# Decay on TensorE for three batches, and GpSimd in place of the DMA queue for the other five

## The chip, the cores and the metric

The kernel runs on one core of a Trainium2 chip. The metric is device time in microseconds. A core has engines that run side by side, each through its own list of instructions in order: TensorE (matrix products; PE in the profile, PEld its weight loads), VectorE (DVE), ScalarE (ACT), GpSimd (POOL) and SyncE (SP). In this kernel SP's queue starts most DMAs, and 16 DMA engines move the data. SBUF is the working memory with 128 partitions, PSUM the memory into which TensorE writes.

## The reference

Attention with a decay, then a gated product of the tokens with weights:

```python
scores = (1 / sqrt(64)) * q @ k.T                  # 8 batches, 8 heads, 576 positions, 64 wide
cum = cumsum(log(clip(f, 1e-4, 1.0)), axis=-1)     # one row of 576 for each of 64 heads
scores = where(j > i, -1e9, scores + cum[i] - cum[j])
attn = softmax(scores)                              # over j
x = (attn @ v), the heads side by side              # 4608 tokens x 512
out = ((x @ w_a) * (x @ w_b)) @ w_out               # 512 -> 1536 -> 512
```

Because the softmax is taken over j, the term cum[i] falls out, and only -cum[j] has to be added to a score. For that, the vector cum of a head has to be there on all the partitions that hold that head's queries: it has to be spread.

## The kernel before, in words

A batch is worked in four **pairs** of heads; pair number t runs from 0 to 31, so batch b has t = 4b to 4b+3, and a **unit** u is two pairs. The queries of a head fall into blocks i = 0 to 3 of 128 and a last one, i = 4, of 64. A block i sees the keys of blocks 0 to i.

For each unit TensorE forms the scores in four groups (`qk_group`, L379): blocks 1 and 0, block 2, block 3, block 4. What follows depends on the batch.

- **Batches 0 and 1** (`DIRECT = 2`): the decay is added by TensorE too, as matmuls with a one-column selector (`pick`) against rows of cum in fp16 (`crow`), and the causal mask by matmuls of `low` with `neg`, into the same PSUM tile (L398 to L428). VectorE then takes the row maximum from PSUM (`do_max`, L484), and ScalarE the exponential from PSUM (L537, L543).
- **Batches 2 to 7**: a DMA on SP's queue reads two rows of cum from `cum_d` in HBM and writes them to all 128 partitions of a buffer `spread` (`load_spread`, L451). GpSimd makes masked copies of it with three affine selects (L458, L464, L469). VectorE adds scores and spread decay and takes the extremum in one instruction for each block and head (`do_decay`, L508) into an SBUF tile `S`, from which ScalarE takes the exponential.

In both cases ScalarE also sums the rows, VectorE takes reciprocals (L550, L552), and GpSimd multiplies each block by them in place (`do_norm`, L560: a `tensor_scalar` whose scalar is a column of `st`). The normalised blocks are turned by TensorE in batch 0 and by transposing DMAs on SP's queue (L576) from batch 1 on; TensorE multiplies them with v (L604, L606, L616, L629) into `xT`. GpSimd also converts k, q and v (L141, L139) to fp16.

The second product is made in tiles of 256, 256, 256, 384, six times 512, and 384 tokens: for each of 12 blocks of 128 columns two groups of matmuls (`psa`, `psb`, L877), a copy of the one (ScalarE or VectorE) and VectorE's product (L888), and then the matmuls `pso` (L897). A tile needs the attention of all heads of its tokens.

The order is written out by hand: every step is an `op` with a number, `ORDER` lists all numbers, and `CHOICE` gives the engine where more than one may do it. An engine's own list is `ORDER` cut down to that engine, and nothing overtakes within it. In it TensorE's matmuls of the second product for earlier tokens stand between the attention steps of later batches. The last products with v (t = 30, 31) stand behind all but the last two token tiles of TensorE's list.

The cum rows themselves come from a start section (L190 to L226): f is loaded twice by two DMAs, once as the first 16 heads four times over on partitions 0 to 63, once as all 64 heads on partitions 64 to 127; then clip, logarithm, scan, and two VectorE steps and a copy that make the fp16 rows `crow` of high and low parts.

Of the kernel before, what the change touches and what calls it, by code (L numbers as in the profile page):

```python
# [37 lines left out]
def kernel(  # L38
# [30 lines left out]
    DIRECT = 2  # L69
    EARLY = 2  # L70
    PSPREAD = range(DIRECT * NP, EARLY * NP)
# [13 lines left out]
    lsel = fixed("lsel", [128, 1], FP32)  # L85
# [5 lines left out]
    crow = spare[1][:, 1536:1536 + S]  # L91
# [4 lines left out]
    chigh = wout16.rearrange("p n k -> p (n k)")[:, 4608:4608 + S]  # L96
# [21 lines left out]
    osb_pool = pool("osb", RING["osb"])  # L118
    ps = pool("ps", 1, space=bass.MemoryType.PSUM)
# [37 lines left out]
    def picks(_):  # L157
        nc.vector.tensor_reduce(out=lsel, in_=ident.rearrange("p (a x r) -> p x a r", x=2, r=16)[:, 1],
                                axis=AXXY, op=ADD, negate=True)
# [25 lines left out]
    def f_tiles():  # L185
        x = [s_pool.tile([128, 1024], FP32, tag="S", name=n) for n in ("cum_f", "cum_l")]
        cw["f"], cw["l"] = x[0][:, 0:S], x[1][:, 0:S]
# [15 lines left out]
    def clip(lo, hi):  # L203
        x = cw["f"][:, lo:hi]
        nc.vector.tensor_scalar(out=x, in0=x, scalar1=1e-4, scalar2=1.0, op0=MAX, op1=MIN)
# [4 lines left out]
    def scan(lo, hi):  # L210
        x = cw["f"]
        nc.vector.tensor_tensor_scan(out=x[:, lo:hi], data0=cw["1"][:, lo:hi], data1=cw["l"][:, lo:hi],
                                     initial=x[:, lo - 1:lo] if lo else 0.0, op0=MUL, op1=SUB)

    def high_part(lo, hi):
        nc.vector.tensor_copy(out=chigh[HP[0], lo:hi], in_=cw["f"][HP[0], lo:hi])

    def rows_part(lo, hi):
        nc.vector.scalar_tensor_tensor(out=crow[HP[0], lo:hi], in0=chigh[HP[0], lo:hi], scalar=lsel[HP[0]],
                                       in1=cw["f"][HP[0], lo:hi], op0=MUL, op1=ADD)  # L220

    def rows_again(e, lo, hi):
        ENG[e].tensor_copy(out=crow[HP[1], lo:hi], in_=crow[HP[0], lo:hi])

    def cum_store(_):
        nc.sync.dma_start(out=cum_d, in_=cw["f"][HP[1]])  # L226

    f_tiles()
    o_f = [op("AS", "ldf", lambda e, m=m: f_load(e, m), size=m) for m in range(2)]
    s_users = [take(o_f[0], "S") for _ in range(2)]  # L230
    o_f[1].after.append(o_f[0])
    o0 = op("D", "ones", f_ones, [])
    o0.after.append(o_f[0])
    o_w = op("A", "table", warm_table(LN), [o0])
    crow_ops, lns, mine = [], [], [o_f[1], o0]
    for lo, hi in ((0, 256), (256, S)):
        a = (lo, hi)
        o1 = op("D", "fclip", lambda _, a=a: clip(*a), o_f, hi - lo)
# [3 lines left out]
        o4 = op("D", "fhi", lambda _, a=a: high_part(*a), [o3], hi - lo)  # L242
        o5 = op("D", "frow", lambda _, a=a: rows_part(*a), [o4, o_pick], hi - lo)
        crow_ops.append(op("DP", "frow2", lambda e, a=a: rows_again(e, *a), [o5], hi - lo))
# [27 lines left out]
    def load_qk(b, which, hh):  # L272
        if b == 0 and hh:
            c = wout16.rearrange("p n k -> p (n k)")[:, 2304 * (which == "q"):2304 * (which == "q") + 2304]
            x = c.bitcast(FP32)
# [21 lines left out]
    def batch_inputs(b):  # L297
# [4 lines left out]
        for which, part, gm in items:  # L302
            gate = qk_ops[(2 * (b - 1) + gm // 4, gm % 4)][-1:] if b else []
# [17 lines left out]
            ld = op("S", "ldqk", lambda _, which=which, hh=hh: load_qk(b, which, hh))  # L321
# [3 lines left out]
            for lo, hi in (((0, 5), (5, TW)) if b == 0 else ((0, TW),)):  # L325
# [5 lines left out]
                else:  # L331
                    ca.deps.append(cas[0])
                    nx.append(ca)
                cas.append(ca)
            tp = op("D", "tqk", lambda _, which=which, hh=hh: transpose_qk(b, which, hh), cas)
# [3 lines left out]
            else:  # L339
                tp.deps.append(T_ops[(which, b, 0)])  # L340
# [6 lines left out]
    def weights():  # L347
# [8 lines left out]
        for nm, js, src, dst, n in items:  # L356
            o = op("P", "ldw", lambda _, src=src, dst=dst: nc.gpsimd.dma_start(out=dst, in_=src), size=n)
            if nm == "o":
                o.deps.extend([*crow_ops, T_ops[("q", 0, 1)], T_ops[("k", 0, 1)]])
# [19 lines left out]
    def qk_group(u, g):  # L379
        b, hh = divmod(u, 2)  # L380
        qT, kT = T[("T", "q", b)], T[("T", "k", b)]
        if single(u, g):
# [3 lines left out]
        heads = [(c[w] if g == 3 else [c[w][0], c[w][1]] if single(u, g) else [c[w][:, 0, :], c[w][:, 1, :]],  # L386
                  h, RG[2 * w + h], 8 * b + 4 * hh + 2 * w + h) for w in range(2) for h in range(2)]
# [4 lines left out]
        if g == 3:  # L392
# [4 lines left out]
            for x, lo, hi in ((0, 0, SF), (1, SF, S)):  # L397
                if b < DIRECT or (b < EARLY and x):  # L398
                    for y, h, r, n in heads:
                        mm(y[HP[h], x, 0:hi - lo], pick[r, n:n + 1].to_broadcast([32, 64]), crow[r, lo:hi], stop=True)  # L400
            if b < EARLY:
# [8 lines left out]
        for i in groups[g]:  # L410
# [718 lines left out]
```

## Time and profile before

| | us |
|---|---|
| median of three runs | 405.43 (403.7 to 407.23) |
| the profiled execution | 402.69 |
| its span, first to last instruction | 400.9 |
| TensorE busy | 378.9 (95%) |
| VectorE busy | 315.5 (79%) |
| GpSimd busy | 262.8 (66%) |
| ScalarE busy | 250.6 (63%) |
| moved by DMA | 80.71 MB, of which 24 spread loads of 576 KB |

The span is about 2 us shorter than the execution's own time. Busy time leaves out instructions that an engine's sequencer does by itself. In a row of the profile, L560 is line 560 of the kernel, "PA<-PA,st" the written and the read tiles, "x60" a count, then come the busy time in us and the mean of one in ns, and behind the bar the idle time of that engine just before these instructions. A row of a table of stretches gives, for each engine, its busy time within the stretch and the number of its instructions, then the granted TensorE clock, the share of the 16 DMA engines (queued packets count, so it can pass 1) and GB/s.

### The profile page before, as it was taken

To read this page: it belongs to the slowest core of one execution; us is meant where nothing else is said; L and a number is where in the kernel's file an instruction comes from. 1 tells how busy PE (TensorE), PEld (TensorE's weight loads), DVE (VectorE), ACT (ScalarE), POOL (GpSimd) and SP (SyncE) were. 2 spreads that over 40 slices of the span, in tenths; PEclk is the share of its full clock that TensorE was granted. 3 is DMA by queue.
4 is the path that set the end of the run, shared out by engine and by line. 5 is a ranking of instruction groups with operands and counts; after the bars stand their busy time and mean duration, and the time that the engine had idled before them with its cause. 6 is when DMAs were issued, how large, how long until landed. Compare 5 with 4: busy or idle time off the path is not lost.

```text
span 400.9 us, 10798 instructions
## 1 busy us (share of the span) xinstructions
PE 378.9 (95%) x3856; PEld 209.3 (52%) x3856; DVE 315.5 (79%) x958; ACT 250.6 (63%) x756; POOL 262.8 (66%) x438
## 2 busy tenths in 40 slices
PE   5679799989999999999999999999999999999996
PEld 5557575765846544444545454544454444444553
DVE  5879997979998988989899789899959893373450
ACT  2678895768768777758785777675868673310111
POOL 4988899787967796979696948697858753000000
PEclk9869999999999999999999999999999999999999
DMA  7999999999999999999899998999997827101102
GB/s 245 261 217 224 253 284 224 233 209 225 208 281 224 267 199 305 202 310 191 270 217 286 238 301 168 242 242 243 255 199 192 151 68 177 54 0 53 55 2 78
DMA packets 149466, 80.71 MB, mean 201 GB/s; under 512 B 130660, under 2 KB 133476, under 8 KB 149412
## 3 DMA queue, kind: packets, MB, share of 16 engines
q1 hardware_dynamic: 145492, 75.02, 79.1%
q0 software_dynamic: 3696, 4.72, 7.0%
q8 instruction: 30, 0.49, 0.5%
q10 hardware_dynamic: 224, 0.28, 0.2%
q14 instruction: 24, 0.20, 0.1%
HBM read 52.20 MB, written 9.58 MB: 154 GB/s over the span
## 4 chain that ended last, share of the span: by engine, by line
PE 69%; DMA 8%; DVE 8%; POOL 5%; ACT 4%; issue 4%; SPq 0%; POOLq 0%; ACTq 0%; DVEq 0%
PE psb L877 20%; PE psa L877 20%; PE pso L897 16%; PE sc L390 7%; DVE st L484 3%; PE pv L604 2%; DMA PTB<-PB 2%; POOL PA L560 2%; DMA spread<-cum_d 2%; DMA k<-in_k_dram 2%; PE idle L174 1%; DVE ht L888 1%; DVE S L508 1%; DMA out_dram<-osb 1%; DMA xT<-PA 1%
## 5 line engine op out<-in xcount | busy, mean ns | idle before, releaser
L877 PE MATMUL psb<-xT,wb 128*128 128x512 f16 (+2 forms) x528 | 115.2, 341 | 2.4 <-DVE a L141 1.3
L877 PE MATMUL psa<-xT,wa 128*128 128x512 f16 (+2 forms) x528 | 115.2, 341 | 0.5 <-ACT osb L137 0.2
L508 DVE CUSTOM_DVE_ANT_0 S<-sc,spread 128x128 f32<-128x128 f32 (+3 forms) x192 | 104.3, 567 | 7.8 <-PE sc L390 6.7
L560 POOL TENSOR_SCALAR PA<-PA,st 128x128 f16<-128x128 f16 (+2 forms) x180 | 84.4, 482 | 33.8 <-DVE st L552 19.8
L897 PE MATMUL pso<-wout,ht 128*128 128x512 f16 (+1 forms) x444 | 98.4, 374 | 0.0
L888 DVE TENSOR_TENSOR ht<-psb,a 128x512 f16<-128x512 f32 (+2 forms) x132 | 76.7, 588 | 14.1 <-PE psb L877 10.1
L543 ACT ACTIVATE PA<-S,st 128x256 f16<-128x256 f32 (+2 forms) x144 | 71.9, 501 | 22.9 <-DVE st L508 21.4
L877 PEld LDWEIGHTS <-wb 128*128 128x128 f16 x528 | 49.8, 98 | 45.7 <-issue 6.8
L877 PEld LDWEIGHTS <-wa 128*128 128x128 f16 x528 | 50.4, 98 | 42.7 <-issue 2.0
L560 POOL TENSOR_SCALAR PB<-PB,st 128x512 f16<-128x512 f16 (+1 forms) x90 | 62.8, 712 | 10.6 <-DVE st L552 5.9
L897 PEld LDWEIGHTS <-ht 128*128 128x128 f16 x444 | 41.8, 98 | 48.1 <-issue 2.8
L137 ACT CAST a<-psa 128x512 f16<-128x512 f32 (+2 forms) x85 | 42.7, 511 | 34.8 <-PE psa L877 33.4
L390 PE MATMUL sc<-kT,qT 32*128 32x128 f16 (+5 forms) x960 | 41.3, 272 | 6.8 <-DVE qT L294 4.6
L543 ACT ACTIVATE PB<-S,st 128x512 f16<-128x512 f32 x48 | 34.3, 716 | 8.1 <-DVE st L508 7.4
L484 DVE TENSOR_REDUCE st<-sc 128x1 f32<-128x576 f32 (+8 forms) x48 | 31.4, 693 | 6.8 <-PE sc L390 5.2
L141 DVE CAST a<-psa 128x512 f16<-128x512 f32 (+2 forms) x47 | 26.2, 558 | 11.3 <-PE psa L877 10.8
L390 PEld LDWEIGHTS <-qT 32*128 32x128 f16 (+1 forms) x960 | 19.0, 96 | 28.8 <-issue 12.3
L552 DVE RECIPROCAL st<-st 128x2 f32<-128x2 f32 x128 | 18.6, 157 | 11.5 <-ACT PB L543 6.1
L537 ACT ACTIVATE PB<-S,st 128x576 f16<-128x576 f32 x24 | 18.6, 775 | 13.9 <-DVE st L508 5.0
L543 ACT ACTIVATION_READ_ACCUMULATOR PA<-S,st 128x1 f32 x144 | 27.2, 189 | 0.0
L137 ACT COPY osb<-pso 128x512 f32<-128x512 f32 (+1 forms) x26 | 14.4, 563 | 20.3 <-PE pso L897 18.6
L141 POOL CAST k<-k 128x1152 f16<-128x1152 f32 (+2 forms) x16 | 22.1, 1384 | 5.0 <-DMA k<-in_k_dram 5.0
(87 smaller groups left out, 449.8 us busy)
## 6 DMA issues: line engine op xcount, KB each, us to landing
spread<-cum_d SPq DMA_DIRECT2D x24, 576.0 KB, 5.9
out_dram<-osb SPq DMA_DIRECT2D x35, 256.0 KB, 4.0
k<-in_k_dram SPq DMA_DIRECT2D x15, 576.0 KB, 6.5
q<-in_q_dram SPq DMA_DIRECT2D x15, 576.0 KB, 6.9
v<-in_v_dram SPq DMA_DIRECT2D x32, 256.0 KB, 6.7
wout<-in_moe_w_out_dram POOLq DMA_DIRECT2D x3, 512.0 KB, 11.0
wa<-in_moe_w_a_dram POOLq DMA_DIRECT2D x1, 1024.0 KB, 13.9
v<-in_v_dram SPq DMA_DIRECT2D x8, 128.0 KB, 6.0
```

What stands on the lines that cost most here:

```text
L137: nc.scalar.copy(out=out_, in_=in_)
L141: ENG[e].tensor_copy(out=out_, in_=in_)
L390: nc.tensor.matmul(out=dst, lhsT=lhsT, rhs=rhs, start=start, stop=stop, skip_group_check=True)
L484: nc.vector.tensor_reduce(out=m if i == 4 else st[:, 2 * i:2 * i + 2][:, h:h + 1] if isinstance(x, list) else m, in_=y, axis=AXX, op=MAX, ...
L508: nc.vector.tensor_tensor_reduce(out=o, in0=x, in1=y, scale=-1.0, scalar=3e38, op0=ADD, op1=MIN, accum_out=m)
L537: nc.scalar.activation(out=p_blocks(t, 4), in_=T[("s" if direct else "z", t, 4)], func=EXP, bias=st[:, 8:9], scale=sign, accum_out=st[:, 1 ...
L543: nc.scalar.activation(out=p_blocks(t, i)[:, :, h, :], in_=x.rearrange("p (j k) -> p j k", k=128), func=EXP, scale=sign, bias=st[:, c:c + ...
L552: nc.vector.reciprocal(out=st[:, 20 + 2 * i:22 + 2 * i], in_=st[:, 10 + 2 * i:12 + 2 * i])
L560: ENG[e].tensor_scalar(out=p, in0=p, scalar1=st[:, c:c + 1], scalar2=1.0, op0=MUL, op1=MUL)
L877: nc.tensor.matmul(out=p[:, 0:n], lhsT=w16[:, db, 128 * fb:128 * fb + 128], rhs=xTflat[db][:, t0:t0 + n], start=(db == 0), stop=(db == 3))
L888: nc.vector.tensor_tensor(out=ht[:, 0:n], in0=T.pop(("psb", t0, fb))[:, 0:n], in1=T.pop(("a16", t0, fb))[:, 0:n], op=MUL)
L897: nc.tensor.matmul(out=o, lhsT=T[("ht", t0, fb)][:, 128 * tb:128 * tb + 128], rhs=wout16[:, fb, c], start=(fb == 0), stop=(fb == 11))
```

## The change

- **f and cum.** f is loaded once, 64 heads on 64 partitions. The scan runs on those 64. The fp16 rows are made as a high and a low part of the first 32 heads (`parts`), and TensorE spreads them with a selector `sel` to two tiles `crow[0]` (batches 0 and 1) and `crow[1]` (batch 2), which ScalarE or VectorE takes out of PSUM.
- **Three direct batches.** `DIRECT = 3`: batch 2 too has its decay and masks from TensorE, and its maximum and exponential are taken from PSUM. Its four spread loads, 12 affine selects and 40 `do_decay` instructions go.
- **GpSimd spreads the decay of batches 3 to 7.** A small DMA for each unit brings four rows of cum to partitions 0, 32, 64 and 96 of a new tile `rw`; for each pair GpSimd issues two `partition_broadcast` instructions, of 576 fp32 each, into `spread`. The affine selects of these batches stay as they are.
- **Batch 1 by blocks.** It takes batch 0's order of work (`attention_by_blocks`: each group for both units before the next), with P tiles of t = 6 and 7 in `spread` buffers and of t = 5 in an `S` buffer. Its P tiles are still turned by DMA; the buffers of its two A parts are now counted apart.
- **Small.** `st` has 8 buffers (6), `ht` 13 (14), and a tile of 256 tokens puts two blocks in one `ht` buffer. Loads of q, k and v for batch 1 no longer wait for named groups of scores. A form of the token tile for 128 tokens from two batches (`PAIR`) is written but no tile has that size.
- **Order.** `ORDER` and `CHOICE` are new throughout: 2321 steps where there were 2342.

In the new lists GpSimd has 20 spreading steps (`bcp`, two broadcasts each). Cut down to GpSimd, a typical stretch reads (steps with their pair; mc, mt and ml are the affine selects, ca the conversions):

```
cak b5, cav b4, bcp t20, bcp t21, mc t21, mc t20, norm0 t18, norm1 t18, norm1 t18, norm0 t19, ...
norm3 t19, norm3 t19, norm4 t19, bcp t23, caq b5, bcp t22, cak b5, norm1 t20, norm1 t21, ...
```

The diff, cut to its core:

```diff
-    DIRECT = 2
+    DIRECT = 3
+    SETS = (DIRECT + 1) // 2
     EARLY = 2
-    PSPREAD = range(DIRECT * NP, EARLY * NP)
...
-    crow = spare[1][:, 1536:1536 + S]
+    crow = [spare[n][:, 1536:1536 + S] for n in (1, 3)]
...
-    chigh = wout16.rearrange("p n k -> p (n k)")[:, 4608:4608 + S]
+    sel = spare[2][0:32, 1536:2048].rearrange("p (c e m) -> p c e m", c=2, e=2)
+    parts = wout16.rearrange("p n k -> p (n k)")[0:32, 4608:4608 + 2 * S].rearrange("p (e s) -> p e s", e=2)
...
-    RING = {"S": 2, "bc": 4, "n32": 3, "n16": 2, "PA": 3, "PB": 2, "PTA": 2, "PTB": 2, "st": 6, "ht": 14, "a16": 3, "osb": 2, "ff": 4}
+    RING = {"S": 2, "bc": 4, "n32": 3, "n16": 2, "PA": 3, "PB": 2, "PTA": 2, "PTB": 2, "st": 8, "ht": 13, "a16": 3, "osb": 2, "ff": 4, "rw": 1}
...
-    HOME = {2: 1, 3: 2}
+    HOME = {2: 1, 3: 2, 6: 3, 7: 0}
+    IN_S = (5,)
...
+        nc.vector.memset(sel, 0.0)
+        for c in range(SETS):
+            for e in range(2):
+                nc.vector.tensor_copy(out=sel[:, c, e].rearrange("p (g e r) -> p g e r", e=2, r=16)[:, :, e],
+                                      in_=eye[0:32, 16 * c:16 * c + 16].unsqueeze(1).to_broadcast([32, 4, 16]))
...
-    def f_load(e, m):
-        rows = f.rearrange("b h s -> (b h) s")
-        if m == 0:
-            rows = bass.AP(rows.tensor, 0, [[0, 4], [S, 16], [1, S]])
-        ENG[e].dma_start(out=cw["f"][HP[m]], in_=rows)
+    def f_load(e):
+        ENG[e].dma_start(out=cw["f"], in_=f.rearrange("b h s -> (b h) s"))
...
-    def high_part(lo, hi):
-        nc.vector.tensor_copy(out=chigh[HP[0], lo:hi], in_=cw["f"][HP[0], lo:hi])
-
-    def rows_part(lo, hi):
-        nc.vector.scalar_tensor_tensor(out=crow[HP[0], lo:hi], in0=chigh[HP[0], lo:hi], scalar=lsel[HP[0]],
-                                       in1=cw["f"][HP[0], lo:hi], op0=MUL, op1=ADD)
-
-    def rows_again(e, lo, hi):
-        ENG[e].tensor_copy(out=crow[HP[1], lo:hi], in_=crow[HP[0], lo:hi])
+    def high_part(e, lo, hi):
+        cast(e, parts[:, 0, lo:hi], cw["f"][0:32, lo:hi])
+
+    def low_part(e, lo, hi):
+        ENG[e].tensor_tensor(out=parts[:, 1, lo:hi], in0=cw["f"][0:32, lo:hi], in1=parts[:, 0, lo:hi], op=SUB)
+
+    def rows_mm(n, lo, hi):
+        c = T[("rows", n, lo)] = ps.tile([128, 512], FP32, tag="ff", bufs=RING["ff"], name="rows")
+        for e in range(2):
+            nc.tensor.matmul(out=c[:, 0:hi - lo], lhsT=sel[:, n, e], rhs=parts[:, e, lo:hi], start=e == 0, stop=e == 1)
+
+    def rows_ev(e, n, lo, hi):
+        cast(e, crow[n][:, lo:hi], T.pop(("rows", n, lo))[:, 0:hi - lo])
 
     def cum_store(_):
-        nc.sync.dma_start(out=cum_d, in_=cw["f"][HP[1]])
+        nc.sync.dma_start(out=cum_d, in_=cw["f"])
...
+        o5 = op("DP", "flo", lambda e, a=a: low_part(e, *a), [o4], hi - lo)
+        for n in range(SETS):
+            bm = op("E", "crep", lambda _, n=n, a=a: rows_mm(n, *a), [o4, o5, o_pick], hi - lo)
+            us = take(bm, "ff")
+            crow_ops[n].append(op("AD", "cev", lambda e, n=n, a=a: rows_ev(e, n, *a), [bm], hi - lo))
+            us.append(crow_ops[n][-1])
...
-            gate = qk_ops[(2 * (b - 1) + gm // 4, gm % 4)][-1:] if b else []
+            gate = qk_ops[(2 * (b - 1) + gm // 4, gm % 4)][-1:] if b >= EARLY else []
...
             if b < DIRECT:
-                for y, h, r, n in heads:
-                    mm(y[h][:, base:col], pick[r, n:n + 1].to_broadcast([32, 128]), crow[r, 0:col - base], stop=True)
-            if b < EARLY and i == groups[g][-1]:
+                at = base
+                for j0, j1 in key_runs(t0, i):
+                    n0 = at
+                    at += 128 * (j1 - j0)
+                    for y, h, r, n in heads:
+                        mm(y[h][:, n0:at], pick[r, n:n + 1].to_broadcast([32, 128]), rows[r, 128 * j0:128 * j1], stop=True)
+            if b < DIRECT and i == groups[g][-1]:
                 m = len(groups[g])
+                lo = 0 if turned(t0, groups[g][0]) else col - 128 * m
+                hi = 128 if m == 1 and lo == 0 else col
                 for a in range(4):
                     for y, h, r, _ in heads:
-                        x = y[h][:, col - 128 * m:col].rearrange("p (m k) -> p m k", k=128)[:, :, 32 * a:32 * a + 32]
-                        mm(x, low[r, a, :], neg[r, :].unsqueeze(1).to_broadcast([32, m, 32]), stop=True)
+                        x = y[h][:, lo:hi].rearrange("p (m k) -> p m k", k=128)
+                        x = x[:, 0:3:2] if hi - lo == 384 else x
+                        mm(x[:, :, 32 * a:32 * a + 32], low[r, a, :], neg[r, :].unsqueeze(1).to_broadcast([32, m, 32]), stop=True)
...
-    def spread_mm(t):
-        b, pr = divmod(t, NP)
+    def load_rows(u):
+        x = T[("rw", u)] = rw_pool.tile([128, S], FP32, tag="rw", name="rw")
+        nc.sync.dma_start(out=x.rearrange("(h r) s -> h r s", r=32)[:, 0, :], in_=cum_d[4 * u:4 * u + 4, :])
+
+    def spread_rows(t):
         for h in range(2):
-            c = T[("scd", t, h)] = ps.tile([128, 512], FP32, tag="ff", bufs=RING["ff"], name="scd")
-            n = 8 * b + 2 * pr + h
-            nc.tensor.matmul(out=c, lhsT=pick[RG[h], n:n + 1].to_broadcast([32, 128]), rhs=crow[RG[h], 0:512],
-                             start=True, stop=True)
-
-    def spread_ev(e, t, h):
-        cast(e, spread[t % RING["bc"]][:, h, SM:SM + SF], T.pop(("scd", t, h)))
-
-    def spread_tail(t):
-        nc.gpsimd.memset(spread[t % RING["bc"]][:, :, SM + SF:SM + S], 0.0)
-
-    def load_spread(t):
-        nc.sync.dma_start(out=spread[t % RING["bc"]][:, :, SM:SM + S],
-                          in_=cum_d.rearrange("(n h) s -> n (h s)", h=2)[t:t + 1, :].to_broadcast(
-                              [128, 2 * S]).rearrange("p (h s) -> p h s", h=2))
+            nc.gpsimd.partition_broadcast(spread[t % RING["bc"]][:, h, SM:SM + S], T[("rw", t // 2)][RG[2 * (t % 2) + h], :])
...
+        if ("P", "A", t) not in T and t in IN_S:
+            x = s_pool.tile([128, 1024], FP32, tag="S", name="S").bitcast(FP16)
+            T[("P", "A", t)] = x[:, 0:12 * 128].rearrange("p (n k) -> p n k", k=128)
...
-        ld = op("S", "ldb", lambda _: load_spread(t), [o6])
+        u = t // 2
+        if t % 2 == 0:
+            rw_ops[u] = op("S", "ldr", lambda _: load_rows(u), [o6])
+            rw_users[u] = take(rw_ops[u], "rw")
+        ld = op("P", "bcp", lambda _: spread_rows(t), [rw_ops[u]])
+        rw_users[u].append(ld)
...
-    def first_attention():
+    def attention_by_blocks(b):
         st_users, pu, norms = {}, {}, {}
         for t, us in home_users.items():
             pu[("A", t)] = pu[("B", t)] = us
         for g in range(4):
-            for u in range(2):
-                deps = [T_ops[(x, 0, u)] for x in "qk"] + [o_low, o_pick] + crow_ops[:1 if g == 0 else 2]
+            for u in (2 * b, 2 * b + 1):
+                deps = [T_ops[(x, b, u % 2)] for x in "qk"] + [o_low, o_pick] + crow_ops[0][:1 if g == 0 else 2]
...
+    def turns(b, part):
+        return (b, part) in {(0, "A0"), (0, "A1"), (0, "B")}
...
-                        if la is None:
-                            la = take(took, f"LA{pr}")
-                        else:
-                            took.after.append(la[0])
-                            la.append(took)
-                        ptu[part] = la
+                        ptu[part] = take(took, f"L{part}{pr}")
...
-        if b == 0:
-            first_attention()
+        if b < EARLY:
+            attention_by_blocks(b)
```

More of the change, by code (lines that the diff above doesn't have):

```diff
@@ L201, in warm_table, with clip @@
         return lambda _: nc.scalar.activation(out=warm, in_=warm, func=func)
-    def clip(lo, hi):
+    def clip(e, lo, hi):
         x = cw["f"][:, lo:hi]
-        nc.vector.tensor_scalar(out=x, in0=x, scalar1=1e-4, scalar2=1.0, op0=MAX, op1=MIN)
+        ENG[e].tensor_scalar(out=x, in0=x, scalar1=1e-4, scalar2=1.0, op0=MAX, op1=MIN)
     def log(lo, hi):
@@ L331, in batch_inputs @@
                 else:
-                    ca.deps.append(cas[0])
+                    ca.after.append(cas[0])
                     nx.append(ca)
                 cas.append(ca)
-            tp = op("D", "tqk", lambda _, which=which, hh=hh: transpose_qk(b, which, hh), cas)
+            tp = op("D", "tqk", lambda _, which=which, hh=hh: transpose_qk(b, which, hh), cas, TW)
             nx.append(tp)
@@ L339, in batch_inputs @@
             else:
-                tp.deps.append(T_ops[(which, b, 0)])
+                tp.after.append(T_users[(which, b)][0])
                 T_users[(which, b)].append(tp)
@@ L381, in qk_group @@
         qT, kT = T[("T", "q", b)], T[("T", "k", b)]
+        rows = crow[b // 2] if b < DIRECT else None
         if single(u, g):
@@ L790, in first_attention @@
                     softmax(2 * u + w, g, qk, sc[w], None, st_users, pu, norms)
-        for t in range(NP):
+        for t in range(NP * b, NP * b + NP):
             values(t, pu, norms)
+    def turns(b, part):
+        return (b, part) in {(0, "A0"), (0, "A1"), (0, "B")}
     def values(t, pu, norms):
@@ L796, in values @@
         early = b < EARLY
-        trs, ptu, la = {}, {}, None
+        trs, ptu = {}, {}
         for part in ("A0", "A1", "B") if early else ("A", "B"):
@@ L903, in ff_ocopy, with ff_store @@
         T[("osb", t0, tb, c)] = osb
-    def ff_store(e, t0, tb, c):
+    def ff_store(e, t0, n, tb, c):
         r0 = t0 + 128 * tb
+        if n == PAIR:
+            x = T.pop(("osb", t0, tb, c))
+            for b in range(2):
+                ENG[e].dma_start(out=out[S * b + r0:S * b + r0 + 64, c], in_=x[HP[b], 0:c.stop - c.start])
+            return
         ENG[e].dma_start(out=out[r0:r0 + 128, c], in_=T.pop(("osb", t0, tb, c))[:, 0:c.stop - c.start])
@@ L916, in ffn @@
         need = set()
-        for tok in range(t0, t0 + n, 64):
+        for tok in (t0, S + t0) if n == PAIR else range(t0, t0 + n, 64):
             b, i = tok // S, (tok % S) // 128
@@ L932, in ffn @@
             mu = op("D", "mul", lambda _, fb=fb: ff_mul(t0, n, fb), [mb, ca], n)
-            hu = take(mu, "ht")
+            if n > 256 or fb % 2 == 0:
+                hu = take(mu, "ht")
+            else:
+                hu.append(mu)
+                mu.after.append(hu[0])
             ub.append(mu)
```

189 lines of the change are left out of this document (88 added, 101 removed), and 130 rows, old and new, of the table ORDER.

## The prediction, as it stood before the result

> **What bounds the kernel now.** I read the busy times first, then the slices, then the chain that ended last.
>
> ```profile
> span 400.9 us, 10798 instructions
> ...
> PE 378.9 (95%) x3856; PEld 209.3 (52%) x3856; DVE 315.5 (79%) x958; ACT 250.6 (63%) x756; POOL 262.8 (66%) x438
> ...
> PE   5679799989999999999999999999999999999996
> ...
> POOL 4988899787967796979696948697858753000000
> ...
> DMA  7999999999999999999899998999997827101102
> ...
> PE 69%; DMA 8%; DVE 8%; POOL 5%; ACT 4%; issue 4%; SPq 0%; POOLq 0%; ACTq 0%; DVEq 0%
> PE psb L877 20%; PE psa L877 20%; PE pso L897 16%; PE sc L390 7%; DVE st L484 3%; PE pv L604 2%; DMA PTB<-PB 2%; POOL PA L560 2%; DMA spread<-cum_d 2%; DMA k<-in_k_dram 2%; PE idle L174 1%; DVE ht L888 1%; DVE S L508 1%; DMA out_dram<-osb 1%; DMA xT<-PA 1%
> ```
>
> TensorE leads: 69% of the chain. But three others are close behind. The DMA row stands at 8 or 9 up to the 30th slice, and GpSimd at 4 to 9 until its work ends in the 34th. So I cut the span where GpSimd's part in it changes, and look at when its work is done.
>
> ```profile
> 0.00:65.00 65.00, 50.95 (x882) 40.84 (x883) 53.64 (x129) 44.73 (x134) 53.23 (x89) 0.92 1.05 245
> 65.00:336.00 271.00, 266.76 (x2619) 137.01 (x2617) 236.81 (x789) 195.55 (x601) 209.59 (x350) 1.00 0.99 226
> 336.00:401.00 65.00, 61.15 (x359) 31.43 (x356) 25.09 (x42) 10.31 (x21) 0.00 (x0) 0.99 0.17 54
> ```
> ```profile
> 334.44 1.36 POOL L560 TENSOR_SCALAR PB<-PB,st 128x512 f16<-128x512 f16 x2 [1.05 <-DVE st L552]
> ```
>
> The columns after the times are PE, PEld, DVE, ACT, POOL. In the long middle stretch, 65 to 336 us, TensorE is busy 266.8 of 271 us and GpSimd 209.6, so GpSimd has 61 us to spare. The last scaling of P ends at 335.8 us. What follows, 65 us, is nearly all TensorE: the last products with v and the two token tiles that need the last batch. In both orders these two tiles stand behind the products with v of t = 30 and 31, so I carry the 65 us over.
>
> **What the change costs GpSimd.** These are the rows.
>
> ```profile
> L458 POOL TENSOR_SCALAR_AFFINE_SELECT spread<-spread 128x768 f32<-128x768 f32 x24 | 20.8, 867 | 3.3 <-DMA spread<-cum_d 3.3
> L469 POOL TENSOR_SCALAR_AFFINE_SELECT spread<-spread 128x256 f32<-128x256 f32 x24 | 9.8, 409 | 2.2 <-DVE st L508 2.1
> L464 POOL TENSOR_SCALAR_AFFINE_SELECT spread<-spread 128x128 f32<-128x128 f32 x24 | 6.9, 295 | 10.1 <-DMA spread<-cum_d 10.1
> L560 POOL TENSOR_SCALAR PB<-PB,st 128x576 f16<-128x576 f16 x30 | 22.4, 748 | 4.3 <-DVE st L550 3.3 <-ACT PB L543 0.5 <-issue 0.4
> L141 POOL CAST k<-k 128x1152 f16<-128x1152 f32 x14 | 19.6, 1397 | 0.0
> ```
>
> *Taken away:* batch 2's affine selects, 4 x (0.867 + 0.409 + 0.295) = 6.3 us. *Added:* 20 pairs x 2 = 40 broadcasts of 576 elements. The trace has none. Below stands the 256-element select (0.41 us), above the conversion of 1152 elements (1.40 us); I take the row with the same 576 elements, 0.75 us, so 30.0 us (16.4 to 55.9). That alone fits into the 61 us.
>
> *Added as well: changes of GpSimd's code.* [...] In the new GpSimd list I count the places where it passes from a `tensor_scalar` to a broadcast or back: 16 stretches of broadcasts, so **32 changes**. Four pairs of steps share a stretch (t = 20 and 21, for instance); elsewhere a scaling or a conversion of q stands between, as between t = 23 and t = 22. What does one cost?
>
> ```profile
> masks.py:199 POOLq MODIFY_POOL_CONFIG  x2: 13/13/13, 2.4 to 2.4; - x2
> ```
> ```profile
> 2.52 0.29 POOL masks.py:199 TENSOR_SCALAR_AFFINE_SELECT ident<-ident 128x128 f16<-128x128 f16 x1
> ```
> ```profile
> L201 ACT ACT_TABLE_LOAD x2 | 2.6, 1283 | 1.3 <-PEq L1113 1.3
> ```
> ```profile
> v<-in_v_dram SPq DMA_DIRECT2D x8, 128.0 KB, 6.0
> wout<-in_q_dram SPq DMA_DIRECT2D x1, 576.0 KB, 9.0
> wa<-in_moe_w_a_dram POOLq DMA_DIRECT2D x1, 1024.0 KB, 13.9
> ```
>
> Before has such a pair of records once, ahead of its first select, which starts 0.1 us later: there the code was evidently in place. That is the low end, 0.03 us. ScalarE's change of table, 1.28 us, is a load into an engine. The high end is the longest load of the page, 13.9 us. [...] 32 x 6.0 = 192 us (1 to 445). None of it is covered: the scalings behind a change wait for it, the transposing DMAs for the scalings, TensorE's products with v for these, and TensorE's list lets nothing pass.
>
> [...] By the two records of before, if every change were like that one, it would be 1 us.
>
> **The rest of the change.**
>
> ```profile
> L508 DVE CUSTOM_DVE_ANT_0 S<-sc,spread 128x128 f32<-128x128 f32 (+3 forms) x192 | 104.3, 567 | 7.8 <-PE sc L390 6.7
> L484 DVE TENSOR_REDUCE st<-sc 128x1 f32<-128x576 f32 (+8 forms) x48 | 31.4, 693 | 6.8 <-PE sc L390 5.2
> ```
> ```profile
> 13.34 1.12 PE sc L390 x40
> ```
> ```profile
> 252.41 6.40 DMA spread<-cum_d
> ```
> ```profile
> spread<-cum_d SPq DMA_DIRECT2D x24, 576.0 KB, 5.9
> cum_f<-in_f_dram ACTq DMA_DIRECT2D x1, 144.0 KB, 2.7
> ```
> ```profile
> DMA packets 149466, 80.71 MB, mean 201 GB/s; under 512 B 130660, under 2 KB 133476, under 8 KB 149412
> ```
> ```profile
> L219 DVE SCALAR_TENSOR_TENSOR xT<-wout,lsel,cum_f 64x256 f16<-64x256 f16 x1 | 0.7, 716 | 0.0
> L223 POOL COPY xT<-xT 64x256 f16<-64x256 f16 x1 | 0.4, 393 | 0.4 <-DVE xT L219 0.4
> ```
>
> - *Batch 2 on TensorE:* per unit 32 matmuls of the decay and 56 of the masks, so 176; 40 score matmuls took 1.12 us on the chain, so 176 x 0.028 = 4.9 us. On VectorE 40 decays of about 0.57 us give way to 20 maxima of about 0.69: 9 us less. The scores stay in PSUM until the exponential is done; a wait of TensorE for that is worth 0 to 1 us a group, 0 to 8 us for its eight groups, and I take 0, since while GpSimd leads TensorE waits for it anyway.
> - *Spread loads:* all 24 of 576 KB go, 14 of 80.7 MB; on the chain one of 6.4 us is seen.
> - *Start:* where VectorE's step (0.72) and the copy (0.39) stood come a subtraction, two small matmuls and a copy out of PSUM: 1.1 us against about the same, taken as 0 (-1 to +2).
> - *Batch 1 by blocks, buffers, loads without gates, the new order:* all of it moves waits of TensorE in the first 65 us, where it is idle for 14 us; at best these 14 go, at worst as many come; taken as 0.
> - *New waits:* each broadcast waits for the small load of its unit and for the decays that last read its buffer; behind it in the queue stand the scalings of the unit before. The load is issued right behind the q load that the conversion just ahead of the broadcast needs, so I take 0 (up to 2.7 us each, the first load of f).
>
> **The sum.** GpSimd's work in the middle stretch becomes 209.6 - 6.3 + 30.0 + 192 = 425.3 us, and GpSimd leads there instead of TensorE. The first broadcast stands as step 64 of 433 in its list, among batch 1's scalings, about where I cut at 65 us. GpSimd will still wait a little; of its 61 idle us now I keep 20 (0 to 61), because the changes give the exponentials time to be ready. 65 + 425.3 + 20 + 65 = 575.3 us span; with the 1.8 us that the profiled execution (402.7) has around its span 577, and since the median of the runs shown is 2.7 us over that execution, **580 us**.
>
> **Rivals.**
>
> - *A change costs as little as a table load.* With 1.28 us each GpSimd's work is 209.6 - 6.3 + 30 + 41 = 274.3, and 65 + 274 + 20 + 65 + 4.5 = 429 us, 6% slower. For it: it is the one load into an engine in the trace. [...]
> - *Changes cost nothing, and the DMA relief counts (faster).* This is the mechanism that the description aims at: the DMA engines are at 0.99 to 1.05 and the chain has 8% DMA, 32 us. GpSimd then has 233 us of work in 271, and TensorE leads again. The spread piece goes, -6.4; of the other 25.6 us of DMA pieces a share like that of the bytes, 14/80.7, -4.5; batch 2's matmuls +4.9: 405.4 - 6 = 399 us. For it speaks the pair of records of before, with nothing behind it. It decides at (271 - 233 - 20)/32 = 0.6 us a change: dearer, and GpSimd leads.
> [...]
>
> **Chances and range.** Forecast, a change between about 2 and 9 us: 0.70. Table-load price, 0.6 to 2 us: 0.15. Free: 0.10. Over 9 us: 0.05. The range goes from the table price with no idle time, 409, to the 9 us price, 676; the broadcast's own bounds (-14 to +26 us) lie inside. Left out are the free and the dearest case, 0.15. About 1% is what a measurement of this kernel can tell from no change (the three runs span 0.9%). Faster by more: 0.07 and the same: 0.04, from the free case and the foot of the next; slower: 0.89.
>
> **What would show it.** In the trace after: some 64 MODIFY_POOL_CONFIG records on GpSimd's queue, each pair followed by a gap of 4 to 8 us in which no GpSimd instruction runs and "issue" is the cause; broadcasts of about 0.75 us; TensorE idle for a third of the middle stretch, on P's transposes and products with v; DMA engines at 0.6 or less there; the chain led by GpSimd. [...] What would make the sum wrong is above all the price of one change: every microsecond is 32 in the time.

## The result

The changed kernel takes 608.97 us (median; 605.9 to 612.13) where the kernel before takes 404.56 us: 1.505 times as long, with an interval of 1.4988 to 1.5112. The prediction was 580 us, with a range of 409 to 676. The profiled execution took 605.9 us, its span is 604.0 us.

### The profile page after: what moved, and what is told of

The parts are those of the page before. It is cut to its first block, busy times and chain, and to the rows that moved or that the text cites. A ratio compares the mean times of both kernels' runs of the same rounds, so it can differ in the third digit from the quotient of the medians.

```text
span 604.0 us, 11142 instructions
## 1 busy us (share of the span) xinstructions
PE 424.6 (70%) x4040; PEld 225.2 (37%) x4040; DVE 313.8 (52%) x905; ACT 252.6 (42%) x758; POOL 285.0 (47%) x465
## 5 line engine op out<-in xcount | busy, mean ns | idle before, releaser
L514 DVE CUSTOM_DVE_ANT_0 S<-sc,spread 128x128 f32<-128x128 f32 (+3 forms) x160 | 87.7, 567 | 130.5 <-POOL spread L475 86.9
L879 PE MATMUL psb<-xT,wb 128*128 128x512 f16 (+2 forms) x528 | 126.7, 366 | 22.3 <-ACT a L139 20.2
L879 PE MATMUL psa<-xT,wa 128*128 128x512 f16 (+2 forms) x528 | 126.8, 367 | 18.4 <-DVE ht L895 15.4
L552 ACT ACTIVATE PA<-S,st 128x256 f16<-128x256 f32 (+2 forms) x120 | 60.1, 503 | 59.7 <-DVE st L514 59.5
L460 POOL PARTITION_BROADCAST spread<-rw x40 | 31.7, 862 | 106.4 <-issue 84.5
L490 DVE TENSOR_REDUCE st<-sc 128x2 f32<-128x512 f32 (+8 forms) x68 | 46.7, 725 | 13.1 <-PE sc L400 9.9
L143 DVE CAST a<-psa 128x256 f16<-128x256 f32 (+2 forms) x52 | 28.6, 549 | 23.3 <-PE psa L879 22.8
L303 DVE STREAM_TRANSPOSE qT<-q 128x576 f32<-128x576 f32 x16 | 19.3, 1206 | 29.1 <-POOL q L141 29.1
L141 POOL TENSOR_SCALAR q<-q 128x1152 f16<-128x1152 f32 (+1 forms) x15 | 20.3, 1351 | 19.8 <-issue 15.3
L303 DVE STREAM_TRANSPOSE kT<-k 128x576 f32<-128x576 f32 x16 | 19.3, 1209 | 17.5 <-POOL k L143 17.4
```

The lines of the kernel that those rows point to most:

```text
L143: ENG[e].tensor_copy(out=out_, in_=in_)
L303: nc.vector.transpose(out=y.rearrange("p (a s w) -> p w a s", a=2, s=NSLOT), in_=x.rearrange("p (w a d) -> p w a d", a=2, d=32))
L460: nc.gpsimd.partition_broadcast(spread[t % RING["bc"]][:, h, SM:SM + S], T[("rw", t // 2)][RG[2 * (t % 2) + h], :])
L490: nc.vector.tensor_reduce(out=m if i == 4 else st[:, 2 * i:2 * i + 2][:, h:h + 1] if isinstance(x, list) else m, in_=y, axis=AXX, op=MAX, ...
L514: nc.vector.tensor_tensor_reduce(out=o, in0=x, in1=y, scale=-1.0, scalar=3e38, op0=ADD, op1=MIN, accum_out=m)
L552: nc.scalar.activation(out=p_blocks(t, i)[:, :, h, :], in_=x.rearrange("p (j k) -> p j k", k=128), func=EXP, scale=sign, bias=st[:, c:c + ...
```

## The profile after

The page of the changed kernel, its busy times and its slices:

```profile
span 604.0 us, 11142 instructions
...
PE 424.6 (70%) x4040; PEld 225.2 (37%) x4040; DVE 313.8 (52%) x905; ACT 252.6 (42%) x758; POOL 285.0 (47%) x465
...
PE   8779938883583942905946478856684195999997
...
POOL 6876198422629127226553255382921756540000
PEclk8989968988695975965988578879688598999999
DMA  9998099940726504512915128270761273370011
...
PE 14%; DMA 0%; ACT 0%; issue 0%; ACTq 0%
```

TensorE's row is no longer a wall of nines: it is torn from the sixth slice to the 34th. GpSimd's busy time has hardly grown, from 262.8 to 285.0 us, and at 47% it looks like an engine with time to spare. That is the trap in this page: GpSimd's busy time leaves out the gaps behind the records of its sequencer, and they are nearly as long in sum as all that it does in the middle stretch (220.1 us against 240.2, below). The chain, which was followed back only through the last seventh of the span, does not help. The rows of the broadcast's line show it, with counts, durations in ns (least, median, most) and places:

```profile
L460 POOL PARTITION_BROADCAST spread<-rw x40: 856/862/865, 65.7 to 496.0; - x40
L460 POOLq MODIFY_POOL_CONFIG  x32: 1/4/18, 58.8 to 486.0; - x32
```

and those of the scaling's line and of the conversion of q:

```profile
L569 POOLq MODIFY_POOL_CONFIG  x28: 11/127/127, 67.3 to 496.9; - x28
```
```profile
L141 POOLq MODIFY_POOL_CONFIG  x4: 4/66/127, 122.5 to 329.0; - x4
```

Records come in pairs, so these are 16 changes ahead of a broadcast and 16 back, the 32 that were counted in the order. A change, here and below (in the prediction a change of GpSimd's code), is such a pair with the gap behind it; what the engine does in the gap no run shows. The records themselves take 1 to 127 ns. The gaps stand behind them, in GpSimd's list in order of time (start, duration, what; in brackets the idle time ahead and what ended it):

```profile
112.72 1.39 POOL L143 CAST k<-k 128x1152 f16<-128x1152 f32 x1
120.24 1.60 POOL L460 PARTITION_BROADCAST spread<-rw  x2 [6.13 <-issue]
121.91 0.60 POOL L143 CAST nv<-v 64x512 f16<-64x512 f32 x1
130.59 1.40 POOL L141 TENSOR_SCALAR q<-q 128x1152 f16<-128x1152 f32 x1 [8.08 <-issue]
139.49 1.60 POOL L460 PARTITION_BROADCAST spread<-rw  x2 [7.50 <-issue]
148.16 2.15 POOL L569 TENSOR_SCALAR PA<-PA,st 128x384 f16<-128x384 f16 x4 [7.07 <-issue]
```

For 1.60 us of broadcasting GpSimd stands still for 6 to 8 us on either side. "issue" as the cause means that nothing the profile shows held the instruction. A plain conversion (121.91) starts 0.07 us behind the end of a broadcast, and so do the affine selects that stand right behind one (0.07 to 0.08 us, six times). Measured from the record to the next instruction of the engine, the 32 gaps are 103.3 us for the 16 ways in (5.7 to 7.5 each) and 116.8 us for the 16 ways back (6.8 to 8.1): 220.1 us, 6.9 a change.

The stretches, cut where the first change begins and just behind GpSimd's last instruction, which ends at 537.3 us (PE, PEld, DVE, ACT and POOL busy, then clock, DMA share, GB/s):

```profile
0.00:59.00 59.00, 48.93 (x805) 39.22 (x806) 50.68 (x123) 45.35 (x137) 44.78 (x75) 0.94 0.99 228
59.00:540.00 481.00, 315.04 (x2883) 154.76 (x2882) 236.78 (x739) 197.99 (x604) 240.20 (x390) 0.81 0.48 104
540.00:604.00 64.00, 60.61 (x356) 31.20 (x354) 26.31 (x44) 9.29 (x18) 0.00 (x0) 1.00 0.14 50
```

The whole loss is in the middle: 481 us instead of 271. 240.2 busy and 220.1 in gaps leave GpSimd 20.7 us of other idle time there, 2.7 of them behind its last instruction: it is the engine that hardly rests.

How does a pause of GpSimd reach TensorE? The longest waits (engine and line, what it waited for, us in total, times, longest):

```profile
PE sc L400 <- DVE st L514: 99.0, 20, 15.5
POOL PA L569 <- issue: 94.6, 13, 8.1
ACT PB L552 <- DVE st L514: 91.7, 12, 20.8
DVE S L514 <- POOL spread L475: 86.9, 10, 20.5
POOL spread L460 <- issue: 84.5, 13, 7.5
```

VectorE waits for GpSimd's affine selects (L475), and TensorE and ScalarE wait for VectorE. One place in full, first VectorE's and then TensorE's list:

```profile
139.63 0.56 DVE L895 TENSOR_TENSOR ht<-psb,a 128x384 f16<-128x384 f32 x1
156.59 1.22 DVE L303 STREAM_TRANSPOSE qT<-q 128x576 f32<-128x576 f32 x1 [16.41 <-POOL q L141]
157.65 0.16 DVE L559 RECIPROCAL st<-st 128x1 f32<-128x1 f32 x1
157.67 0.15 DVE L561 RECIPROCAL st<-st 128x2 f32<-128x2 f32 x1
157.74 0.54 DVE L895 TENSOR_TENSOR ht<-psb,a 128x384 f16<-128x384 f32 x1
```
```profile
142.08 0.81 PE L879 MATMUL psb<-xT,wb 128*128 128x384 f16 x4
158.33 1.44 PE L879 MATMUL psa<-xT,wa 128*128 128x384 f16 x4 [15.44 <-DVE ht L895]
```

GpSimd comes out of its change at 148.2 us and works off its scalings; the conversion of q is done at 156.6. VectorE's transpose of q waited for it for 16.4 us, 7.1 of them the gap behind the broadcasts and most of the rest the work that the gap had held up. Behind the transpose, in the same list, stood the product `ht` of a token tile that has nothing to do with q. TensorE needs the PSUM buffer of that product and stops for 15.4 us.

## The experiments

The theory: the time goes by the number of GpSimd's changes, each 6 to 8 us, and by nothing else of the change. The rivals: the new order, the blocks of batch 1 or batch 2 on TensorE cost time by themselves; the broadcasts and their loads cost it; GpSimd's idle time takes up a part.

### The broadcasts as plain copies

```diff
-            nc.gpsimd.partition_broadcast(spread[...][:, h, SM:SM + S], T[("rw", t // 2)][RG[...], :])
+            nc.gpsimd.tensor_copy(out=spread[...][:, h, SM:SM + S], in_=rw)
...
```

> The changed kernel with each broadcast replaced by a plain copy of as many elements (576 fp32) at the same place of GpSimd's list, after the same small loads: the work and the waits stay, the change of code goes. It leaves out the spreading: the decay of batches 3 to 7 is not that of the reference. Theory: 395 to 410 us, GpSimd busy about 285 us, TensorE leads; this is the case in which a change of code is free. Rival (GpSimd's added 30 us, or its waits for the small loads, hold back the others): 430 us or more.

402.0 us against 404.3, 0.995 times (0.992 to 0.998). The group of the copies and the middle stretch of this kernel:

```profile
L461 POOL COPY spread<-rw 128x576 f32<-128x576 f32 x40 | 25.4, 669 | 2.4 <-DMA rw<-cum_d 2.4
```
```profile
65.00:336.00 271.00, 268.51 (x2807) 139.39 (x2807) 230.09 (x724) 193.28 (x584) 228.86 (x382) 1.00 0.85 182
```

GpSimd does about the same work at the same places behind the same small loads (2.4 us of waiting for them in all), and the loss is gone: 207 us of 609 hang on the kind of instruction, of which only 6.3 are the longer busy time of the broadcasts (31.7 us against 25.4). It also shows that the rest of the change, new order and all, does not cost time by itself: with the copies in it the kernel is half a per cent faster than before.

### Nothing but the changes, in the kernel before

```diff
...
+        there = [mc_of[t] for t in [13, 12, 15, 14, 16, 17, 18, 19, 20, 23, 22, 24, 27, 29, 28, 31]]
         for o in order:
+            if o in there:
+                nc.gpsimd.partition_broadcast(tiny[:, 0:8], tiny[0:32, 8:16])
             o.fn(o.eng)
```

> The kernel before, spread DMAs and all, with one broadcast of 8 elements in a scratch tile ahead of the long affine select of the 16 pairs at which the changed kernel enters a stretch of broadcasts: 32 changes of code and nothing else. Theory: GpSimd's 210 us of the middle stretch plus 32 x 6.9 = 220 and about 12 us for the small broadcasts themselves, 442 + 20 idle + 65 + 65 + 4 = 596 us (560 to 620). Rival (what is dear is the 576-element broadcast together with the new order): under 480 us. If a change waits for the DMA engines, which are fuller here, its gap will be longer than 6.9 us.

621.0 us against 404.3, 1.536 times (1.528 to 1.544). Sixteen broadcasts of 8 elements, in the old order, with the old spread DMAs, make the kernel slower than the whole change does. GpSimd's list around one of them, and the middle stretch:

```profile
306.06 0.59 POOL L563 TENSOR_SCALAR PA<-PA,st 128x384 f16<-128x384 f16 x1
312.52 0.28 POOL L1103 PARTITION_BROADCAST tiny<-tiny  x1 [5.87 <-issue]
312.67 0.97 POOL L461 TENSOR_SCALAR_AFFINE_SELECT spread<-spread 128x768 f32<-128x768 f32 x1
320.69 0.94 POOL L563 TENSOR_SCALAR PA<-PA,st 128x128 f16<-128x128 f16 x2 [7.06 <-issue]
```
```profile
65.00:553.00 488.00, 301.27 (x2621) 149.45 (x2620) 239.15 (x790) 197.28 (x601) 214.94 (x367) 0.81 0.55 127
```

The affine select starts 0.15 us after the broadcast's start, with no gap between them; between the select and the scaling behind it stand 7.06 us. The 32 gaps make 211.9 us. 488 - 214.9 - 211.9 leaves GpSimd 61 us of idle time: exactly what it had in the kernel before. None of it went into the changes, and that is why this run lies 25 us over its expectation, just above the range, for the expectation had left only 20 idle: 41 us more of idle time, less 8 us of gaps and some 7 us of small broadcasts that were reckoned too dear.

### Four of them

```diff
-        there = [mc_of[t] for t in [13, 12, 15, 14, 16, 17, 18, 19, 20, 23, 22, 24, 27, 29, 28, 31]]
+        there = [mc_of[t] for t in [16, 20, 24, 28]]
```

> The kernel before with only four of the small broadcasts (ahead of the long affine selects of t = 16, 20, 24 and 28): 8 changes of code, about 8 x 6.6 = 53 us of GpSimd's time, some 50 us apart. If GpSimd's 61 idle us of the middle stretch can take them (the sum of the prediction, in which 20 stay idle), 53 - 41 = 12 us more than before, 416 us. If a pause of 13 us in a queue that keeps its order cannot be made up, nearly all 53 us show: 445 to 458 us.

460.4 us against 404.4, 1.139 times (1.135 to 1.143). Eight changes, 53.4 us of gaps, and 56.0 us in the time. Its middle stretch:

```profile
65.00:394.00 329.00, 278.26 (x2618) 140.68 (x2617) 237.10 (x786) 195.81 (x601) 209.16 (x353) 0.92 0.83 187
```

Here GpSimd is far from full: 329 - 209.2 - 53.4 = 66 us idle. The changes show in full nevertheless. The idle time is spread over more than fifty short waits, none longer than 4.8 us, and TensorE, which before was busy 266.8 of 271 us, has nothing in hand with which to catch up. Its own row splits the 58 us by which the stretch has grown: 46.5 are idle time of TensorE, and 11.5 are busy time for the same work (278.3 instead of 266.8 us), at a granted clock of 0.92 instead of 1.00. So the time lost is close to the time of the gaps only as a sum: about four fifths of it is waiting, the rest TensorE working more slowly.

### Eleven stretches instead of sixteen

```diff
...
+        for t, other in ((12, 15), (17, 16), (19, 18), (22, 23), (28, 29)):
+            seq.remove(bcp_of[t])
+            seq.insert(seq.index(bcp_of[other]) + (t > 12), bcp_of[t])
         return seq
```

> The changed kernel with five spreading steps moved beside another one (t = 12 to 15, 17 to 16, 19 to 18, 22 to 23, 28 to 29), so that GpSimd passes between the two sets 22 times instead of 32. Theory (the time goes by the count of changes): 10 x 6.9 = 69 us less, 540 us (525 to 555). Rival (the time goes by the number of broadcasts or by when they stand in the list): within 15 us of 609.

GpSimd now passes between its `tensor_scalar` instructions and its broadcasts 22 times. 548.4 us, 1.355 times before (1.346 to 1.363), inside the expectation: 60.6 us less than the changed kernel for 10 changes fewer, with the same 40 broadcasts. The middle stretch:

```profile
59.00:480.00 421.00, 310.79 (x2892) 153.37 (x2890) 236.91 (x740) 197.96 (x604) 240.29 (x390) 0.86 0.55 118
```

GpSimd's busy time is that of the changed kernel (240.3 against 240.2); its 22 gaps make 153.5 us instead of 220.1. The time goes by the count:

| kernel | changes | us | over | us a change |
|---|---|---|---|---|
| before, four small broadcasts | 8 | 460.4 | 404.4 (before) | 7.0 |
| before, sixteen | 32 | 621.0 | 404.3 (before) | 6.8 |
| changed, eleven stretches | 22 | 548.4 | 402.0 (copies) | 6.7 |
| changed | 32 | 609.0 | 402.0 (copies) | 6.5 |

### No spreading at all

```diff
         make_identity(nc, ident)
+        for x in spread:
+            nc.gpsimd.memset(x[:, :, SM:SM + S], 0.0)
...
     def spread_rows(t):
-        for h in range(2):
-            nc.gpsimd.partition_broadcast(...)
+        return
```

> The changed kernel with the spreading left out altogether, small loads and broadcasts: the affine selects and decays run on what the buffers hold, so the decay of batches 3 to 7 is not that of the reference. It shows the most that the change could have gained if spreading cost nothing: no reloads, no 14 MB of spread loads, 32 us less on GpSimd than with the copies. If TensorE alone sets the time, it equals the run with copies, 399 to 403 us; if GpSimd's copies held something back, 390 to 398 us.

406.9 us against 402.6, 1.011 times (1.007 to 1.014): not faster, a per cent slower, and outside both stretches of the expectation. With the copies' 25 us of GpSimd taken away, and the small loads, nothing is gained. So GpSimd's work on the spreading was not what the time hung on. But this kernel has an addition of its own: so that the buffers hold something, it clears all four of them at the start. GpSimd's list there, and the first stretch, first of the run with copies, then of this one:

```profile
1.25 4.05 POOL L150 MEMSET spread<- 128x1152 f32 x4
```
```profile
0.00:65.00 65.00, 53.63 (x884) 41.08 (x884) 56.20 (x137) 50.03 (x158) 50.06 (x85) 0.95 0.94 220
0.00:65.00 65.00, 48.94 (x806) 38.47 (x807) 55.15 (x124) 45.78 (x139) 49.76 (x82) 0.89 0.92 215
```

The clearing takes 4.05 us ahead of GpSimd's first conversions (the run with copies clears one tile in 0.58), and after 65 us TensorE has done 78 matmuls fewer. TensorE's busy time there is 4.7 us shorter. So the 4.9 us between this run and the copies probably come from its own start; that was not tested apart. Without them it would stand about where the copies stand, not clearly below.

### The spreading by DMA again, in three places of the queues

First each spread DMA right behind the last reader of its buffer, then at the broadcast's own place, then that with the affine selects moved back, then the same from GpSimd's queue.

```diff
-            nc.gpsimd.partition_broadcast(...)
+        nc.sync.dma_start(out=spread[...][:, :, SM:SM + S], in_=cum_d...to_broadcast(...))
...
-        ld = op("P", "bcp", lambda _: spread_rows(t), [rw_ops[u]])
+        ld = bcp_of[t] = op("S", "bcp", lambda _: spread_rows(t), [rw_ops[u]])
...
```

> The changed kernel with one part undone: the 20 spreads of batches 3 to 7 are DMAs from cum_d again, each issued on SP's queue right behind the last reader of its buffer; no broadcasts, no small loads. Theory (32 changes of GpSimd's code at about 6.9 us are the whole loss): all of the loss goes, 395 to 415 us, TensorE leads, one pair of MODIFY_POOL_CONFIG records. Rival (the new order, batch 1 by blocks or batch 2 on TensorE cost time themselves): more than 430 us. Rival (the gaps are something else that GpSimd's longer list brings): GpSimd still has gaps of several us with no cause shown.

> As the run with the spreads by DMA again, but each DMA stands on SP's queue at the broadcast's own place in the order, not right behind the last reader of its buffer. That run took 447 us without a single change of code. If its 43 us over before came from SP's queue (a spread that waits for its buffer holds up the loads of q, k and v behind it), this one is faster, 405 to 430 us, though the affine selects now wait for a DMA that has just started. If they came from the new order or from batch 2 on TensorE, it stays at about 447 us.

> As the run with DMA spreads at the broadcasts' places (422 us, where GpSimd waited 28 us for spreads that had just started), with the first two affine selects of each pair moved back in the order, to at most 14 steps ahead of the decay that needs them. If those waits are what is over 404 us, 400 to 412 us; if the selects then come late for VectorE, it stays near 422.

> As the run before in this list, with the spread DMAs started from GpSimd's queue instead of SP's, so that no load or transposing DMA stands behind them. Starting one takes about 0.8 us of GpSimd (the weights' DMAs did), 16 us in all. 398 to 410 us if SP's queue still cost something, 405 to 420 us if not.

Measured: 446.9 us, 1.102 times before (1.093 to 1.110); 422.2, 1.044 (1.041 to 1.048); 424.5, 1.054 (1.049 to 1.059); 421.0, 1.046 (1.043 to 1.049). None has a broadcast on GpSimd, and so none of the 32 passages to one and back, and all are far below 609. But none gets to 404. The first misses its 395 to 415 us and lands where the rival stood (more than 430, because the new order or batch 2 on TensorE cost time); the run with copies, which has both and takes 402 us, speaks against that rival. The second lies inside its 405 to 430. The third misses its 400 to 412 and stays near 422, the fourth lies just over its 405 to 420.

What holds the first back shows in SP's own waits:

```profile
SPq L458 <- DVE st L514: 37.4, 11, 13.8
```

L458 is the spread DMA: it stood at the head of SP's list for up to 13.8 us until VectorE had read its buffer, with the loads of q, k and v and the transposing DMAs behind it. At the broadcast's place this wait is gone, and 25 us with it; there GpSimd's selects wait for a DMA that has just started:

```profile
POOL spread L464 <- DMA spread<-cum_d: 28.1, 7, 8.5
```

Moving the selects back takes these waits away (in the third run no select waits for a spread DMA), and yet the time stays: these waits alone did not set it. Another queue did not help either. What the remaining 18 us over before are stays open. About 10 of them, at the broadcast's place, are a longer busy time of TensorE (391.8 us against 381.7 in the run with copies, at a granted clock of 0.97 against 0.99). The order was laid out for a spread that is there 1.6 us after it starts, and an order laid out for the DMA was not tried.

### The spreading by VectorE

```diff
-            nc.gpsimd.partition_broadcast(spread[...][:, h, SM:SM + S], T[("rw", t // 2)][RG[...], :])
+            nc.vector.stream_shuffle(spread[...][:, h, SM:SM + S], T[("rw", t // 2)], [2 * (t % 2) + h] * 32)
...
```

> The changed kernel with the spreading given to VectorE: the small load puts the four rows of a unit at the head of each quarter of the partitions, and one shuffle for each head (576 fp32) takes the place of each broadcast at its place in the order. [...] Theory: the loss goes, 395 to 412 us; 40 shuffles of about 0.65 us put 26 us on VectorE, GpSimd is 32 us lighter than in the run with copies. Rival (VectorE, at 78% of the span, becomes the bound): 415 us or more.

422.2 us, 1.046 times before (1.041 to 1.051). The group, and the busy line and the chain of the page:

```profile
L462 DVE STREAM_SHUFFLE spread<-rw 128x576 f32<-128x576 f32 x40 | 30.3, 810 | 0.0
```
```profile
PE 389.9 (93%) x4040; PEld 214.5 (51%) x4040; DVE 338.4 (81%) x985; ACT 252.5 (60%) x758; POOL 254.3 (61%) x426
...
PE 59%; DVE 25%; ACT 6%; issue 5%; POOL 2%; DMA 1%; SPq 1%; DVEq 0%; ACTq 0%
```

Without broadcasts on GpSimd nearly all of the loss is gone here too, but the time is the rival's (415 us or more): VectorE, which had 8% of the chain before, now has 25%, and 18 us remain over before for 30 us of shuffles (0.81 us each; the 0.65 of the expectation no run shows). That the shuffles are what these 18 us come from is read off the chain and was not tested apart. No version that computes the decay beat the kernel before.

## Why the prediction was right, step by step

- **What leads, and the count.** As predicted, GpSimd takes the lead in the middle stretch without being busy (240.2 of 481 us), through 32 changes. The count was read from the order alone and holds exactly: the 64 records stand where GpSimd passes from a `tensor_scalar` to a broadcast or back, and none stands ahead of an affine select or a plain conversion but the pair at the start.
- **The price of a change.** Chosen 6.0 us, from the smallest load of the page that repeats; measured 6.9. This is the term that was mis-sized: 220 us instead of 192 is 28 of the 29 us between 580 and 609. That a change takes the time of a load no run shows; what the runs showed is a gap of 5.7 to 7.5 us on the way to a broadcast and of 6.8 to 8.1 on the way back. That the row came so near is luck: a DMA of 128 KB stood in for it, and nothing in the runs ties the two together (the queues that carry instructions move no more packets after than before). The row of the 576 KB load, 9.0, and that of the table load, 1.28, did enclose what was measured.
- **The broadcasts.** Chosen 0.75 us; 0.862 each, two in 1.60. 31.7 us busy instead of 30.0.
- **The ends.** 59 us ahead of the first change instead of 65, 67 behind the last scaling instead of 65. GpSimd's busy time in the middle is 240 instead of 233, since the cut lies earlier. With the idle time below these nearly cancel.
- **The idle time that stays.** Chosen 20 of 61, measured 18 up to GpSimd's last instruction in the changed kernel. The number held by luck, for the reason given did not: "the changes give the exponentials time to be ready" would hold for the kernel before as well, and there all 61 us stayed with 32 changes, and 66 with 8. The run with copies has 38 us idle from 65 us to its last instruction at 332, so the changed kernel had less of it to begin with and gave up about half. Which waits those were was not looked into.
- **The way to TensorE.** Predicted through scalings, transposing DMAs and products with v. The longest waits go another way: GpSimd's selects and conversions hold VectorE's decays and transposes, and VectorE's list, which keeps its order, holds the products of the token tiles.
- **The free rival.** 399 us was predicted for changes that cost nothing; the run with copies has 402.0. But its working was off in parts: 10.9 us were to come from 14 MB less of DMA and 4.9 to go into batch 2's matmuls. The run with copies moves those 14 MB less, has 2.8 us more of TensorE busy time (381.7 against 378.9) and is 2.3 us faster, so an estimate from these numbers leaves some 5 us for the DMA, half of what was reckoned. Its point of decision, 0.6 us a change, was wrong as well: it took GpSimd's idle time for spare time, and eight changes with 53 us of gaps, which its 61 us of idle time would have held, cost 56 us.
- **What was to be seen.** 64 records besides the first pair, gaps of 4 to 8 us with "issue" (5.7 to 8.1), TensorE idle for a third of the middle (481 - 315 = 166 us, 35%), DMA at 0.6 or less (0.48): all there, though what TensorE waits for is mostly something else, as said above. That the chain would name GpSimd could not be checked, as it breaks off.

## What to carry to other kernels

Before moving another kind of instruction to GpSimd, look in a trace for pairs of MODIFY_POOL_CONFIG records with a gap behind them, see between which kinds of instructions they stand, and count in the order how often the engine passes from one to the other: here a passage between a `tensor_scalar` and a broadcast cost about 7 us, for a broadcast of 8 elements (6.6 on average) as for one of 576 (6.9), so a broadcast of 0.9 us among scalings costs 15. Read an engine's list in time, not its busy share: an engine at 47% was the one that held all others. And where the leading engine has nothing in hand (TensorE, busy 266.8 of 271 us), idle time of another engine is not spare time: here a pause of 13 us in a list that keeps its order came out at the end as 14 us, TensorE's slower work behind it included.

## What was not expected of the hardware

- **The way back is dearer** than the way in: 7.3 us on average against 6.5, and so in the other runs (7.6 and 6.4 with eleven stretches, 7.1 and 6.1 in the kernel before with sixteen small broadcasts, 7.2 and 6.1 with four).
- **A change does not show among the DMAs.** The packets of the queues that carry instructions are as many after as before (23 and 31 against 24 and 30), so if a change fetches something, these queues do not show it; what fills the gap stays open. And full DMA engines stretch it little: with the DMA share at 0.02 or less over the five us from its start, a change back took 6.8 to 7.6 us. With the share at 0.8 to 0.9 it took 8.1 at most in the changed kernel and 8.7 in the one with eleven stretches.
- **TensorE's clock falls with the pauses.** In the middle stretch the granted clock is 1.00 in the run with copies, 0.92 with 8 changes, 0.86 with 22 and 0.81 with 32; right behind the pause of 15.4 us shown above, four matmuls took 1.44 us that took 0.81 ahead of it. How much of it shows in the time was not tested apart. Where GpSimd leads it need not; with 8 changes TensorE's 11.5 us more of busy time lie inside the 56.
